# Filling work dealt in another order, with evacuations on either of two engines

## The chip, the core and the metric

The kernel runs on one core of one Trainium2 chip. Its time is the device time of one execution in microseconds (us). Before the change, three runs gave a median of 1594.99 us (1594.81 to 1596.23).

## What is computed

The input `x` has 2048 rows of 512 numbers. Two branches are computed from it and mixed row by row with a gate:

```python
g = _sigmoid((x * gate_w).sum(-1, keepdims=True))
a = _A_ref(x, A_wq, A_wk, A_wv, A_wo)   # attention: 32 query heads of 16, one shared key and value head
b = _B_ref(x, w_gate, w_up, w_down)     # (sigmoid(x @ w_gate) * (x @ w_up)) @ w_down, inner width 1792
return g * a + (1 - g) * b
```

In the attention each query row is compared with all 2048 keys: `softmax(q k / 4) v`, and the heads' results go through `wo`. Branch `b` needs no result of the attention, so its matmuls can be put anywhere between those of the attention; the kernel calls them the filling.

## The kernel before

**Units.** The rows are split in four blocks of 512 (`NB`), and the 32 heads in eight groups of four (`NG`). One block with one group is a unit; there are 32 (`NU`). A unit takes 64 matmuls for the maxima of its scores (`maximum`, L1103, whose result VectorE reduces out of a PSUM bank), 64 for the scores again, the other way up (`scores`, L1112, whose exponential ScalarE takes out of a bank), and 16 value steps (`pv`, L992), each of four narrow matmuls that add exp(scores) times values into one bank.

**The filling.** `block_jobs` (L88) lists it for each block of rows: for each of seven pairs of columns a gate job `g` and an up job `u` (24 matmuls on each half of TensorE), and output jobs `d`, four for each group of pairs in `FG` (L29), that multiply by `w_down`. Jobs `a` multiply the attention result of the block before by `wo`. Before the change the four groups of `d` stand like this: group 0 between `g` and `u` of pair 2 (behind the `a` jobs), group 1 between `g` and `u` of pair 4, groups 2 and 3 in one run at the block's end.

**TensorE in halves.** The matmuls of maxima, scores and filling use 64 rows of the array only; two run side by side, one in the top and one in the bottom half. Such a pair is called a step here. A value step uses the full height.

**The order.** Everything is put in order at build time. `ORDER` (L656) is a text with one sign for each thing that TensorE does next. A hexadecimal digit is a step: its upper and lower two bits say what the top and the bottom half do (0 nothing, 1 a maxima matmul, 2 a scores matmul, 3 a filling matmul). `V` is a value step, `G` a projection group at the start, `T` turns the maxima of a unit, `C` closes the bank of the value sums early, so that the sums go on in another bank, and `.` stands for 25 units of planned waiting. `step` (L624) replays the text in a model, `State`, that keeps a clock for each engine with a table of costs (L40 to L44, in units: a step is 100, a `V` is 371, a reduction on VectorE 260) and so decides at which place the instructions of the other engines, the DMA issues and the GpSimd tasks stand in their queues. Each engine works through its queue in that order; semaphores see to it that nothing is used before it is there.

**Evacuations.** A finished bank is emptied by one engine and then free. Maxima go to VectorE, exponentials, gates and copies to ScalarE, `u` and sums to VectorE. Three things that ScalarE empties matter below: the value sums (`close`, L532, and `sums_out`, L1002: one copy at the end of each unit but the last, which has its own, and one at each `C`); the first part of an output tile, and parts that are added later (`gather`, L432, and `part_of`, L1056: "first" and "apart"). Where a unit's sums come in several copies, GpSimd adds them (`sum_add`, L1005); it also adds the parts that came apart (`add_part`, L1070).

**Buffers.** Eight PSUM banks; two tiles `ou` for the copies of value sums; two buffers `h`; six for the split `hl` (`HB`); four output tiles; two raw buffers for weights on their way in.

Of the kernel before, what the change touches and what calls it, by code (L numbers as in the profile page):

```python
# [11 lines left out]
AF = mybir.ActivationFunctionType  # L12
ALU = mybir.AluOpType
# [8 lines left out]
NT = TB // P  # L22
KC = D // P
# [5 lines left out]
FG = [(0, 2), (2, 4), (4, 5), (5, 7)]  # L29

# [33 lines left out]
M_LEAD, H_LEAD, LOOK = 54, 6, 5  # L64
# [23 lines left out]
def block_jobs(b):  # L88
    out = []

    def ds(gi):
        f0, f1 = FG[gi]
        items = [("d", b, f) for f in range(f0, f1)]
        if gi == len(FG) - 1 and b + 1 < NB:
            items[1:1] = [("x", b + 1, i) for i in range(KC // 2)]
        return [Job("d", b, gi * NT + t, 6 * (f1 - f0), items if t == 0 else ()) for t in range(NT)]

    for gi, (f0, f1) in enumerate(FG):
        for f in range(f0, f1):
            out.append(Job("g", b, f, 24, [("g", b, f)]))  # L100
            if f == f0 and 0 < gi < len(FG) - 1:
                if gi == 1 and b:

                    out += [Job("a", b - 1, t, 3 * KC, [("a", b - 1, i) for i in range(KC // 2)] if t == 0 else ())
                            for t in range(NT)]
                out += ds(gi - 1)
            out.append(Job("u", b, f, 24, [("u", b, f)]))
    return out + ds(len(FG) - 2) + ds(len(FG) - 1)


class State:
# [320 lines left out]
    def gather(self, j, h, i, second, at):  # L432

        key = (j.b, j.i % NT)
        if key not in self.parts:
            self.parts[key] = 1
            n = self.tile_of[key] = self.tile_free.index(min(self.tile_free))
            assert self.tile_free[n] <= self.now
            self.tile_free[n] = NEVER
            self.acts.append(("part", h, j, i, "first"))  # L440
            self.first_at[key] = self.on("act", at, SCALED)
            return self.first_at[key]
        self.parts[key] += 1
# [5 lines left out]
        self.acts.append(("part", h, j, i, "sum"))  # L449
# [6 lines left out]
        return at  # L456

# [74 lines left out]
    def close(self, u, last):  # L532
# [4 lines left out]
        self.acts.append(("sums_out", i, self.sum))  # L537
        at = self.on("act", max(self.now + LATE, self.ou_free[i]), COPY) + TAIL_A
# [142 lines left out]
    "7VV965VVV7a77bf7efededef9bfdbfbf7f6fbdfe7edbbdf6fdV659VV965VVC66f7fe7efbd9fbbfTfff7bfbe7ef7edee7f9ffd5dVVVVC7b7b"
    "7ef6fedbbddbffdfebb7ff6f9fbd6fedffd5dVVVVVC7b7b7e7bfb7bbdbddefb7eb7e7fdefededef9bfdedeVa95VV659VVVCd6fe7ee7fedeb"
    "dbddbfb7ede7fbdeef7bdbff7b7775VVVVVCd9edfef6fe7e7ebd7bfbfTbfb7efdedef9fef977777VVVVC79eefde7f6febdbdfedbdbf9edfe"
    "7fb7bdbf6ff7775VVV6b7b7fb7fbdef9edfed7ddVVVC7adef7bdfbdebd7bfef7dTVVVC66bffdbdf6fbdebd7bfedfefbdfb7fb7ef67ffddaV"
    "VVVVC7b7b97bffedbb7e7fed9feed7fe7edbfe7bf6fafdddVVVVV7b7b7bf9fbdbf6e7fed6fef6ff9bddefe7bedfedf57VVC595VVVC7b7ee7"
    "efdebdbdef7bdbf9fb77efb79fef6bffed9deVV659VV6T9VVC6edf7ebdfbdee7f6f6fbdbdebfdbdfb7bdbedff777aV655VVVV7b7afd7ef9f"
    "6f7bfe7ef9fe7bf6b7ff9defbfeddd5eVVV6a9V9aTVC566VVC7b7bf7bdfbdefeedefdfffedb7efdfef7f7bbV956VVC796ffef9fb7eb7f9ff"
    "dddaVVC5bfb7e7bfbdeede7f6f7ddVVVV7bdef6b7fb7ef9debdf7f7bfbfedeefd9fedbfd77VVVVC66ffbdbdf6febdbdfe7bedfbd6fbdfb7e"
    "dbedff7677VVVa95VVVC6adff7f6fb7bdeedbdfefTefe7bf7edbf9dbfefb77aV95aV555VVVV76b7fbbdfe7eb7f9ef7e7ededfb7bdef9feb7"
    "ffdddaVC6a5VV956VVVC7bde7eb7fb7bf9bdedfefTbfbdfb767efef6fefede5VV95aV969V666V999VVVC79eff67bfbdeede7fede7ef9b7f7"  # L690
    "bbfd6feedff5b7bV95aV59aVV666V996V969V999V666V9a5V9a5V6a9V996VCde6edff6f9fef6fTfbffdbfb7bbdfbde7e7bfff55VVV695VVd"
    "e7e7bb7f9fbf6f9dbf7fb7fbebfdefdededeff57VV656VV6a5VC7a6ff7f6fedaf7fbTfff7bfbedefd9fedef9ff757VVVCde9eedf7fbdbbdd"
    "bf6f777VVCdbb77bfbd9fef6fededd77VVVVC7b7ba7fdfe7afddedefbdef6fbdf6fb7b7e7bfef6ddVVV99aVVVC9bdff6f9fbdbf6bdefd6fe"
    "de7fef6ef7bfTbfbfd775VVVVC766ffeb7fbdeb7dbbfde7b7eb7fe7dbfe7efbddddddVVVVVC5bfe7eedfe7ebd7b7efedebdb7ff9bf7b7b7e"
    "ffddd5VVV6b7ff9f9fedbf67efbd6feVVC7edafdbdfbdebde7fb7e77VV95TVVVC7b6dfeb7fedbf97bfe7f7bffbedf6fedef9f9ff5dVVVVC7"
    "b7ba7fdfedbb7e7e7f9fe7eff6b7f9fedededbff5dVVVVV7bdef6b7fb7bbdbdefdedbedbf77ef6fbdebdef7df9VVC666VV9T5VVC7b7bf9ed"
    "f6fee7edbfdb7bf9f7ef6f9f6fef9fbfd5dVVVVVC7a5ffbb7fedaf7bdf6f9fbf6f7be7efdedbedf9ff5eV965VVVV76efb7defbdef6b7f9f9"
    "fef9fedb7defbdee7fbf577VVV6a9V696V99TVVC7b7bededf9fffbe7bfdfffe7edefdfbfb7ff6VVC6f6f7bbdfb7bf6e7fdddeeVVVCdb9bf7"
    "bdfb7edee7fe7edbVVVV7b7b6fbdfedbdef9fedffbbdefdf9fe7ef6b7fe7bV69aV9a6Va95V6a6Va6aVV9a6VaaaVVaaTVVbaaVVabffebffaf"
    "bVVfeeffbabbbfbcVVeebbbffffffffeeffbfbfebaVVeeaaVVeaeVeeaVaaaVVaaVeeececcceccc8aaV88888VVVV"  # L700
# [11 lines left out]
def tile_kernel(ctx, tc, x_in, wq, wkv, wo, wg, wu, wd, consts_in, out):  # L712
# [289 lines left out]
    def sums_out(i, ps):  # L1002
        nc.scalar.copy(OU[i], ps)  # L1003
# [217 lines left out]
```

## Time and profile before

| what | value |
|---|---|
| median of three runs | 1594.99 us |
| the profiled execution itself | 1595.86 us |
| its span, first to last instruction | 1593.1 us |
| TensorE busy with matmuls | 1585.1 us |
| VectorE busy | 1393.8 us |
| ScalarE busy | 1203.4 us |
| GpSimd busy | 877.9 us |

The profiled execution is 0.87 us above the median, and 2.76 us of it lie outside the span. PE is TensorE, PEld its weight loads, DVE VectorE, ACT ScalarE, POOL GpSimd and SP the engine that issues DMAs. In a list of groups a row gives line, engine, operation, tile written and tiles read, the count, then the time in which any of them ran, the mean duration of one in ns, and after the bar the idle time before them with what ended it. The ends of matmuls are modelled by the profiler; their starts are measured. A maxima, scores or filling matmul is one record; a value step leaves eight records.

### The profile page before, as it was taken

What the parts mean: (1) busy time and instruction counts of PE and PEld (TensorE: products, weight loads), DVE (VectorE), ACT (ScalarE), POOL (GpSimd) and SP (SyncE); (2) the same over time, 40 slices, a digit from 0 to 9 for tenths busy, and PEclk for the clock granted to TensorE, in tenths of its full rate; (3) what the DMA queues carried; (4) which work ended last, traced back from release to release, by engine and by line L of the source; (5) the groups of instructions that cost most, each with busy time, mean ns of one, the idle gap of its engine ahead of it and who ended that gap; (6) DMA issues with size and microseconds to landing.
All of it is one profiled execution on the core that took longest, in us unless ns stands there. A gap on an engine that the chain in (4) does not pass through costs nothing.

```text
span 1593.1 us, 33707 instructions
## 1 busy us (share of the span) xinstructions
PE 1585.1 (99%) x12950; PEld 1001.1 (63%) x12950; DVE 1393.8 (87%) x2420; ACT 1203.4 (76%) x2356; POOL 877.9 (55%) x680
## 2 busy tenths in 40 slices
PE   9999999999999999999999999999999999999998
PEld 7776666556655666665754666666665466666553
DVE  6899999999899998889899989889998998988842
ACT  5277677788788777778778877778778877677797
POOL 5354554666653476567362648285764357656432
PEclk9999999999999999999999999999999999999999
DMA  7312111142111221124011212114211122111011
GB/s 239 139 51 72 39 60 32 32 121 74 38 59 30 77 72 43 34 64 133 27 55 35 72 40 70 36 45 112 84 41 53 32 76 62 51 32 44 9 37 43
DMA packets 52228, 98.10 MB, mean 62 GB/s; under 512 B 17960, under 2 KB 19240, under 8 KB 51044
## 3 DMA queue, kind: packets, MB, share of 16 engines
q1 hardware_dynamic: 52068, 95.96, 20.4%
q8 instruction: 101, 1.65, 0.5%
q14 instruction: 59, 0.48, 0.1%
HBM read 74.05 MB, written 8.90 MB: 52 GB/s over the span
## 4 chain that ended last, share of the span: by engine, by line
PE 99%; ACT 0%; DVE 0%; issue 0%; DVEq 0%; POOL 0%; ACTq 0%; POOLq 0%
PE bank L1087 31%; PE bank L995 30%; PE bank L1108 17%; PE bank L1117 16%; PE bank L849 4%; PE bank L871 0%; ACT p L1119 0%; PE bank L980 0%; PE bank L1160 0%; PE bank L919 0%; ACT x L767 0%; DVE ba L1169 0%; DVEq L1217 0%; POOL v_aug L865 0%; ACT q L941 0%
## 5 line engine op out<-in xcount | busy, mean ns | idle before, releaser
L1110 DVE TENSOR_REDUCE mx<-bank 128x1 f32<-128x512 f32 x2048 | 1261.3, 682 | 133.9 <-PE bank L1108 62.3
L1119 ACT ACTIVATE p<-bank 128x512 f32<-128x512 f32 x2048 | 1043.8, 650 | 85.7 <-PE bank L1117 46.6
L1117 PE MATMUL bank<-qs,ks 64*128 64x512 f32 x2048 | 710.6, 402 | 0.0
L1108 PE MATMUL bank<-ks,qs 62*128 62x512 f32 x2048 | 688.0, 406 | 0.0
L995 PE MATMUL bank<-p,v_aug 128*32 128x512 f32 x4096 | 487.6, 598 | 0.0
L1108 PEld LDWEIGHTS bank<-ks,qs 62*128 62x128 f32 x2048 | 341.1, 185 | 143.7 <-issue 39.2
L1117 PEld LDWEIGHTS bank<-qs,ks 64*128 64x128 f32 x2048 | 352.0, 185 | 107.1 <-DVE mx L1110 33.7
L1087 PE MATMUL bank<-wd,hl 64*128 64x512 f32 x1344 | 265.2, 393 | 0.0
L995 PEld LDWEIGHTS bank<-p,v_aug 128*32 128x32 f32 x4096 | 109.3, 109 | 244.3 <-issue 218.5
L1003 ACT COPY ou<-bank 128x512 f32<-128x512 f32 x112 | 66.2, 591 | 246.3 <-PE bank L995 185.8
L1087 PEld LDWEIGHTS bank<-wd,hl 64*128 64x128 f32 x1344 | 192.3, 185 | 18.9 <-issue 2.5
L1087 PE MATMUL bank<-xs,wu 64*128 64x512 f32 x672 | 188.7, 394 | 0.0
L1087 PE MATMUL bank<-xs,wg 64*128 64x512 f32 x672 | 183.9, 394 | 0.0
L1087 PE MATMUL bank<-x,wu 64*128 64x512 f32 x672 | 183.0, 391 | 0.0
L1087 PE MATMUL bank<-x,wg 64*128 64x512 f32 x672 | 181.6, 391 | 0.0
L1006 POOL TENSOR_TENSOR ou<-ou,ou 128x512 f32<-128x512 f32 x81 | 104.7, 1293 | 137.1 <-ACT ou L1003 136.7
L967 POOL TENSOR_TENSOR qs<-stage,qs 16x1024 fp32r<-16x1024 f32 x62 | 148.4, 2393 | 4.8
L1071 POOL TENSOR_TENSOR ba<-ba,pa_d 128x512 f32<-128x512 f32 x48 | 61.7, 1288 | 116.7 <-DVE ba L1050 77.6
L1087 PEld LDWEIGHTS bank<-x,wg 64*128 64x128 f32 x672 | 112.5, 185 | 10.5 <-issue 0.8
L1087 PEld LDWEIGHTS bank<-xs,wu 64*128 64x128 f32 x672 | 113.1, 185 | 7.9
L1087 PEld LDWEIGHTS bank<-x,wu 64*128 64x128 f32 x672 | 111.7, 185 | 9.6 <-issue 1.7
L1087 PEld LDWEIGHTS bank<-xs,wg 64*128 64x128 f32 x672 | 110.3, 185 | 7.7
(88 smaller groups left out, 1130.1 us busy)
## 6 DMA issues: line engine op xcount, KB each, us to landing
rg<-wg SPq DMA_DIRECT2D x28, 512.0 KB
ru<-wu SPq DMA_DIRECT2D x28, 512.0 KB
rd<-wd SPq DMA_DIRECT2D x28, 512.0 KB
stage<-qd SPq DMA_DIRECT2D x192, 64.0 KB
xs<-x SPq DMA_DIRECT2D x16, 512.0 KB
xf<-x_in SPq DMA_DIRECT2D x16, 256.0 KB
qd<-q SPq DMA_DIRECT2D x16, 256.0 KB
ra<-wo SPq DMA_DIRECT2D x8, 512.0 KB
```

The costliest lines, as they stand in the source:

```text
L849: nc.tensor.matmul(ps, w[:, p, part(kc)], X[b, kc][:, q, :], start=i == 0, stop=i == 3 * KC - 1)
L967: e.tensor_tensor(qs[r], stage[r], f32(qs[r]), op=ALU.subtract)
L995: nc.tensor.matmul(ps[32 * j:32 * j + 32, :], v_aug[:, c, :], PT.pop((u, c, j)), start=new, stop=last)
L1003: nc.scalar.copy(OU[i], ps)
L1006: nc.gpsimd.tensor_tensor(OU[n], OU[n], OU[i], op=ALU.add)
L1071: nc.gpsimd.tensor_tensor(BA[b, t], BA[b, t], PA.pop((b, t)), op=ALU.add)
L1087: nc.tensor.matmul(banks[i], l, r, start=at == 0, stop=at == j.n - 1)
L1108: nc.tensor.matmul(banks[i], qs_t[u % 3][r, pr, part(qt)], ks[r, kb * 512:(kb + 1) * 512], start=True, stop=True)
L1110: nc.vector.tensor_reduce(MX[u][:, pr, h, qt, kb:kb + 1], banks[i], axis=AX.X, op=ALU.max)
L1117: nc.tensor.matmul(banks[i], ks[r, part(c)], qs_t[u % 3][r, pr, :], start=True, stop=True)
L1119: nc.scalar.activation(p, banks[i], AF.Exp, scale=0.25)
```

## The change

Five things change in the planner and in what it emits.

1. `block_jobs` deals the `d` groups by a table `BEHIND`: behind `g` and behind `u` of a pair come two jobs each for groups 1 and 2, all four for groups 0 and 3; the `a` jobs stand behind `g` of pair 2 as before.
2. A function `evacuate` gives the copies of value sums and the "first" and "apart" parts to VectorE or ScalarE, whichever ends earlier by the model's clocks. VectorE's copy is entered with 262 units, its scaled copy with 264; ScalarE's were and are 210 and 247.
3. A copy of value sums is planned to begin 130 units behind the last value step (`LATE_V`), before 190 (`LATE`).
4. `H_LEAD`, by how many matmuls one half of the array may be ahead of the other, goes from 6 to 8.
5. `ORDER` is another text, with the same matmuls. What its signs come to, counted in both texts:

| | before | after |
|---|---|---|
| `V` / `G` / `T` | 512 / 24 / 32 | 512 / 24 / 32 |
| maxima, scores, filling matmuls | 2048, 2048, 4404 | 2048, 2048, 4404 |
| halves that do nothing | 16 | 12 |
| steps (digits) | 4258 | 4256 |
| of these ahead of the first `V` | 108 | 107 |
| runs of `V` | 232 | 230 |
| stretches of steps between runs of `V` | 231 | 229 |
| `C` | 81 | 106 |
| `.` | 0 | 2 |

```diff
+BEHIND = {("g", 2): [(4, 0, 4)], ("u", 2): [(0, 0, 4)], ("g", 4): [(1, 0, 2)], ("u", 4): [(1, 2, 4)],
+          ("g", 5): [(2, 0, 2)], ("u", 5): [(2, 2, 4)], ("u", 6): [(3, 0, 4)]}
...
-M_LEAD, H_LEAD, LOOK = 54, 6, 5
+M_LEAD, H_LEAD, LOOK = 54, 8, 5
+COPY_D, SCALED_D = 262, 264
+LATE_V = 130
...
-    for gi, (f0, f1) in enumerate(FG):
-        for f in range(f0, f1):
-            out.append(Job("g", b, f, 24, [("g", b, f)]))
-            if f == f0 and 0 < gi < len(FG) - 1:
-                if gi == 1 and b:
-
-                    out += [Job("a", b - 1, t, 3 * KC, [("a", b - 1, i) for i in range(KC // 2)] if t == 0 else ())
-                            for t in range(NT)]
-                out += ds(gi - 1)
-            out.append(Job("u", b, f, 24, [("u", b, f)]))
-    return out + ds(len(FG) - 2) + ds(len(FG) - 1)
+    late = [ds(gi) for gi in range(len(FG))]
+    if b:
+        late.append([Job("a", b - 1, t, 3 * KC, [("a", b - 1, i) for i in range(KC // 2)] if t == 0 else ())
+                     for t in range(NT)])
+    for f in range(FG[-1][1]):
+        for kind in "gu":
+            out.append(Job(kind, b, f, 24, [(kind, b, f)]))
+            for gi, first, last in BEHIND.get((kind, f), ()):
+                if gi < len(late):
+                    out += late[gi][first:last]
+    return out
...
-            self.acts.append(("part", h, j, i, "first"))
-            self.first_at[key] = self.on("act", at, SCALED)
+            self.first_at[key], e, _ = self.evacuate(at, SCALED, SCALED_D)
+            self.acts.append(("part", h, j, i, "first", e))
...
-            self.acts.append(("part", h, j, i, "apart"))
-            return self.on("act", max(at, free), SCALED)
+            at, e, _ = self.evacuate(max(at, free), SCALED, SCALED_D)
+            self.acts.append(("part", h, j, i, "apart", e))
+            return at
...
+    def evacuate(self, at, a, d):
+
+        if max(self.dve, at) + d < max(self.act, at) + a:
+            return self.on("dve", at, d), "dve", TAIL + FREE
+        return self.on("act", at, a), "act", TAIL_A + FREE_A
...
-        self.acts.append(("sums_out", i, self.sum))
-        at = self.on("act", max(self.now + LATE, self.ou_free[i]), COPY) + TAIL_A
+        at, e, tail = self.evacuate(max(self.now + LATE_V, self.ou_free[i]), COPY, COPY_D)
+        at += tail - FREE
+        self.acts.append(("sums_out", i, e, self.sum))
...
-        nc.scalar.copy(OU[i], ps)
+        (nc.scalar.copy if e == "act" else nc.vector.tensor_copy)(OU[i], ps)
...
-        nc.scalar.activation(pa, banks[i], AF.Copy, scale=scale[:, n:n + 1])
+        if e == "dve":
+            nc.vector.tensor_scalar(pa, banks[i], scale[:, n:n + 1], None, op0=ALU.mult)
+        else:
+            nc.scalar.activation(pa, banks[i], AF.Copy, scale=scale[:, n:n + 1])
```

The text of `ORDER` (some 4900 signs) is left out of the diff; so are lines that only pass the engine's name on.

More of the change, by code (lines that the diff above doesn't have):

```diff
@@ L446, in gather @@
             self.halves[j.key, "slot"] = slot
-            self.acts.append(("part", h, j, i, "apart"))
-            return self.on("act", max(at, free), SCALED)
-        self.acts.append(("part", h, j, i, "sum"))
+            at, e, _ = self.evacuate(max(at, free), SCALED, SCALED_D)
+            self.acts.append(("part", h, j, i, "apart", e))
+            return at
+        self.acts.append(("part", h, j, i, "sum", "dve"))
         at = self.on("dve", max(at, self.first_at[key]), SUM)
@@ L697 @@
[L697 to L700, printed above, removed]
+    "GGGGGGGG555G555G555G555GG555GG555GGG555GG555G555G555Gdd55GTfffdf777ff7f777ffffffefb7edbf7b7f9fb7efdef79ffedbe7de"
@@ new lines @@
+    "fbde7bbdfed9feffff55VVVC9deefdededefedf6efdb7bdedfdff777777VVVVC97bbfdbdbf77bf7befdedee7fede7ededeffd577VVVC7bTf"
+    "bfb7bfb7b7bfb7e7bdbfb7df577VVVC9dbb7f7bdfdedefbfdbdeff777775VVV6ededfededbfbdedfe7ede7ef6fe7bff55.VVVC6de7bf9fb7"
+    "7bfbffddddd5VVVVC9dedededefeff7f6fb7b7bfeeefTffb7bf767ef77VVC9b7b7b77bfbedfdfdeddddVVVVC6ede7f6fb7edbff6fb7b7ef9"
+    "bf79fbf9f6fedffddd5VVV956VVC97bf9fb7bbdedfedbf7b7e7eedf6febde7f9fefff5TVVVVVC7b76b7fbfbd9fbe7def9fb7bf9ff9edfede"
+    "f6fedf5dVVVVC67b7bbfdb7bedff7fede7e7efbfededfbdef6ff57VVVVV6edef76fbf6efddebf7b7b7b7bfb7afdb7fefededddVVVC6f6def"
@@ new lines @@
+    "edb7b7efbdb7f6fdVV999VVC7e7bf6f6fedb7bedbfdfdTVVVC6deeeddfef6f9ff9dbf6fee7b7fbdef9dbff7bb7777V99aV666V699V659VV6"
+    "eddbfb7b7ddVVC6b7bfdbd7ddeVVC6deedfbdbbdfbddbfbededfb76fefedbdbfe77777VVV67baV95aV9a5V6TaV696VC6f9bfdbdfd7aVVC9d"
+    "eedfeb77b7VVded9bffb79f6fbdefe7b7e7b7ef7ef6f9feb7ffde5dVVC655VVVC6b6ffdedeb7b7fefdefTbfb7bf7b9fededfe7efeb57VV6a"
+    "5V999V699V996V65aV65aV999V656VV9deeddbfde7efeeffb7b7bfbfb7b7e7bfbdffdd5dVVVC69edffedeedfe7f77b7efedebffb7bfdbfbd"
+    "f7757VVVVVC9b77bfe7bdbe7fe7f9fe7beddbfeeTffe7bf7fdedd5VVVVC97bfb7edef9f6f9fedfedef6fbd9fb7ef6f9fff5777VVVV6f6fbd"
@@ new lines @@
+    "9fbf6b7f9ffed6fef9fb7edef75VVC9e9ff76fff5aVVVVCdadff67bfb7bdbedfedb7ef6f7eb7ef7edbf9ff6f5dVVVaaTVVVC9bdfb7bdbf9f"
+    "b77bedfedef9fe7edbbdfedb76fff6dV9a9V696V669V969V666VC699V669VC669V66aV6a5V996V95aV966VCdeTeeff7bf9b7f9f6fed77VVC"
+    "9b77bf9fef9dbf7efed7ddVVVV9e9ffdedef9fbdb7ffde7bfeedefde7ff7b7b7777VVVVC97bfbdb7b7efe76fe7fedbf9def6faf7def9fedf"
+    "f75VVVC7bTbfef9ff9b7fbd9fedddVVVC6b7fe7b7b7bfe7bffb7be7e7e7fefb67VVVC9f9fedb7bf9ef7e7fe7fdddddVVV9e6f7fede7eeVVV"
+    "C99ffb7b7edbbfd7bfe7edeedfede7af7fffddd5VVVVCTeedeffd6f6efedf9fbb7bdfbdededb7bfb7bffb775VVVVC67b7bfe7bb7fb77efe7"
@@ new lines @@
+    "edef6f9f6fedbfdbfdfdddd5VVVVV67b7b7efb7fe7bfdf9f9fbdefbfde7efe7ef7ddddVVVVC6b77bbdfbbdf9fedefdedede7bfbe7deedfbf"
+    "e7b777VVVVC97bfb7efTbfb7bfedeedddVVC97bfb7b7b7eefdeddeffdaV966V666V559VVV7e7ef9f6f6fbde7ebf7ededb7efb7b7fbdbdbdb"
+    "fdddVVC9defb76fe77dVVVC9ededfb7d77bVVC6edf6feb7bdfed7bfb7ef9f6ef7bdbdbb7fbdeffeTdVVC9edfe7bdf775VVV65aVC6b7fedbd"
+    "ebfaVVV9bdfb7bdef9fe7edf9fedef9edfe7af7e7fb7bf5fffed5VVVVVC96f7bf9fb7bb7fededfedede7efedbdbfbb7b777VV666V95aV6Ta"
+    "V696VC95aV65aV696VC67bfe7e7ebddbf9fbfdffedbdef9ffededf7bb777VV9deeeddfbedfdfb7777777VVVVC9b7bf7edbf6bdfbf7ddeddV"
@@ new lines @@
+    "VVC67bfbde7edefedbdbdfb7bb7fb7e7e7efbdedefTff5VVVVVC7b7e7bf9f9f9fe7efe79fef9feddefe7edef7b7bf57VVVVd6fedebdfbd6f"
+    "bdbf6fedbf9dbfedbdfb7ed7f77777VVVVVCTbfedefe7b7bbdf9fb7e7fed9fb7bfe7bbdedfedef6VV996V669V956VVVC9b77ef9fedeedfde"
+    "b7f9fbb7bf7edbf6f9fb76fefddV69aV9a5V669V699V696VC669V969VC966V666VC666V9a5VTa9V9a5VC9f9fbd9fbdee7fe7fb76fdVVC97b"
+    "fb7ededeb7f6fef77ddVVVV9ededfb7ef9bf7dbf9fffededefedef7f7b7b7777VVVVC9b7bb7b7bfdfe7e7fededef9f9feeTffbdbfdb7efd5"
+    "VVVVC6b7b7fb7be7f6fbfbfdb7be7ef79faf7VVVC9e6ff7e7e7efededeffee7edfededf57VV959VVV6dbdbfb7bf7b7bfddededdVVVC67ef6"
@@ new lines @@
+    "f6febddfedebfdbdbdedbfbf9f9e7fff777775VVVVC97bfb79fbf9fede7f9fbfTbfedefdadff6defef7577VVVVC9b7fb7edeedf6fdefedbd"
+    "ef6bdfbdbdbf7e7bff7775VVVVV6b97ffed7be7bff9fed7fbebff7e7fedeedb7f7ddVVVVC97bfededbb7bf7eeddfbededfe7be7f9fedbfe7"
+    "7777VVVVC97efb7edb7bfbddedeffbTVVC9b7fe7e7e7b7bfdeffded5VVVVC9e9f7fb7be7e7fdbe7fbdef6fe7b7eededfb7bdf7ddVV9ede7f"
+    "bdbb7dVVC696V6a5VC97af7fbdbeeeVV9T5VVC7e6fdbdefedef6b7fbd6fbdbbdfb7fedb7bf9fbfed5VVVVC97edef6feb7bVVC9ededefb777"
+    "bVV6f6f6fef6e7edfedfbd9fbbdfb7bdbedbfde7bf5f77VVC655VVVCd9efdebdfbdbb7fb6fdef9fededf6fbdbedbfbb7777VV65aV6a5V9Ta"
@@ new lines @@
+    "V95aVC666V95aV6a5V659VV66ff9f9ff9dbfb7bf7def7bfbfe7efe7ef6e7fdddVVVVC6b7fbd9fef9e7f7bfedffbfbdb7fefTeefdefd677VV"
+    "VVC6deedfb7ef9bfddebfdb7b7bf9fb7ededef9fff7b75VVVVVC97bbfdedbdbfb7edfe7e7ef6f6f9fb7bedfed9fef77VV6a5V655VVVC6ded"
+    "efede7b7efedfb7bdbb7fb7b79feef7edef7fb5V96TVVVVC6f9edfe7edebfddbf9fb7b7bf9fbdedbe7fe7f7ff55VVVVVC9f6fbd9fbf9defd"
+    "bf6f6fbde7efb7bb77bfedefdfd6VC969V966V666V669V699VC699VC65aV669V95aV9TaV966V95aVC97b7bb7bbf7fbf7bdbfe7ef9f6fb7fe"
+    "5VVVC9dedefe7ef6deffbfed9fbf9ffdddddVVV6edededfeedff77b7b7b77VVVVC9f9fb7e7ef6f6f6fbf7b7bbfd6fef6defb7efdeefd5VVV"
@@ L701 @@
+    "b7ef67ef9fbf9dbdbf9fe7bdefedfed6fbf6efd777VVC559VVVC9e9ff7bb7bfTfef6fdf9fadfededfedbf6fefb7b7b5VVVC97e7ef6fef9fb"
+    "ddeff7757VVVVC69f7bf9fe7e7bff9fbf9fefeb7fbdededefedf6bV6b57VVV99fbf7b7bf6ef76feefeee4VC6a6V996V69aV9a9V9a9Vaaa.V"
+    "Va9aVVaTaVaaaVVaaVeeeeeVVbbbffbffbfbbbffbffeeffbbbbaVVaabVVebfeffefefbbbffeaVVeaeeeceVVaaa8VVVVeeeeecccecee8V888"
+    "8VVV"
 )
@@ L1000, in tile_kernel, with sums_out @@
     SUMS = {}
[L1002 to L1003 removed]
+    def sums_out(i, e, ps):
+        (nc.scalar.copy if e == "act" else nc.vector.tensor_copy)(OU[i], ps)
     def sum_add(_, i, n, last):
@@ L1054, in send_out, with part_of @@
         nc.sync.dma_start(out[n * P:(n + 1) * P, :], BA.pop((b, t)))
-    def part_of(h, j, i, how):
+    def part_of(h, j, i, how, e):
         b, t = j.b, j.i % NT
```

45 lines of the change are left out of this document (5 added, 40 removed).

## The prediction

> **What bounds the kernel now.** I read the page's head, its busy row and its chain first, then the list of waits of PE alone.
>
> ```profile
> span 1593.1 us, 33707 instructions
> ...
> PE 1585.1 (99%) x12950; PEld 1001.1 (63%) x12950; DVE 1393.8 (87%) x2420; ACT 1203.4 (76%) x2356; POOL 877.9 (55%) x680
> ...
> PE 99%; ACT 0%; DVE 0%; issue 0%; DVEq 0%; POOL 0%; ACTq 0%; POOLq 0%
> ```
>
> ```profile
> PE bank L871 <- POOL v_aug L865: 1.3, 1, 1.3
> PE bank L1146 <- ACT ou_last L1144: 0.5, 1, 0.5
> PE bank L1155 <- DVE on L1153: 0.4, 1, 0.4
> ```
>
> The chain is TensorE for 99% of the span, and PE's own waits come to 2.2 us, all at the two ends. That alone doesn't settle it: ends of matmuls are modelled, so a short stall can hide in a busy PE. So I price TensorE's work from starts. The next rows are pieces of the chain (start, length): runs of value steps, eight records a step.
>
> ```profile
> 93.52 3.57 PE bank L995 x32
> 107.09 4.43 PE bank L995 x40
> ...
> 1159.76 2.71 PE bank L995 x24
> 1163.37 2.71 PE bank L995 x24
> ```
>
> A run of five steps takes 4.43 us and one of four 3.57: 0.86 us a `V`, and 4.43 - 5 x 0.86 = 0.13 us to get into a run. Between the first two lie 107.09 - 97.09 = 10.00 us. In the text of `ORDER` the first two runs of `V` have 42 steps between them, without a `T`. Between the last two lie 0.90 us, where the text has three steps. A step is (10.00 - 0.90) / 39 = 0.233 us, and getting out of a run costs 0.90 - 3 x 0.233 = 0.20 us. The rows below are windows: the length, then the busy time and count of PE, PEld, DVE, ACT and POOL, clock, DMA share, GB/s.
>
> ```profile
> 97.09:107.09 10.00, 10.00 (x88) 8.14 (x92) 9.60 (x17) 8.64 (x17) 7.18 (x8) 1.00 0.29 91
> 107.09:111.52 4.43, 4.43 (x42) 1.20 (x42) 3.27 (x6) 0.60 (x1) 4.20 (x4) 1.00 0.10 38
> 1162.47:1163.37 0.90, 0.90 (x11) 0.50 (x14) 0.17 (x1) 0.44 (x1) 0.87 (x1) 1.00 0.00 0
> 0.00:93.52 93.52, 92.12 (x497) 71.59 (x501) 72.91 (x133) 41.06 (x72) 38.00 (x30) 1.00 0.54 171
> 93.52:1583.53 1490.01, 1489.68 (x12443) 928.17 (x12443) 1317.85 (x2281) 1160.52 (x2279) 838.64 (x650) 1.00 0.19 54
> 1583.53:1593.14 9.61, 3.29 (x15) 1.37 (x14) 3.06 (x7) 1.86 (x5) 1.27 (x1) 0.90 0.29 109
> ```
>
> The last three cut the span into the head up to the first `V`, the body, and the end behind the last `V`. The body, by the counts of the old text: 512 x 0.86 = 440.3 us, 232 runs x 0.13 = 30.2, 4150 steps (4258 less 108 in the head) x 0.2333 = 968.2, 231 stretches x 0.20 = 46.2. That is 1484.9 of 1490.0. The 5.1 us left hold 31 `T` and every stall there is. **TensorE hardly waits for anyone; the time is the count of its work**, and whatever the other engines gain is worth at most those 5 us.
>
> **The change, part by part.** *The new order on TensorE.* The matmuls are the same. In the body, two runs of `V` and two stretches go, 2 x (0.13 + 0.20) = 0.66 us, and one step (4150 to 4149), 0.23; in the head one step more, 0.23. Two signs `.` come in; at 100 units to a step of 0.233 us, 25 units are 0.06 us each, so 0.12. Sum: -0.66 - 0.23 - 0.23 + 0.12 = **-1.0 us**. `T` and `G` keep their counts. The weights' loads and GpSimd's splits keep theirs and stand elsewhere in their queues; SP's later DMAs stand behind them. I cost this at nothing: the DMA share of the body is 0.19. If that cover failed, TensorE, in order, would stand until the weights are split; no such wait is in its list now.
>
> *More closes.* `C` goes from 81 to 106. With 31 unit ends that makes 137 copies of value sums for 112, and 106 adds on GpSimd for 81.
>
> ```profile
> L1110 DVE TENSOR_REDUCE mx<-bank 128x1 f32<-128x512 f32 x2048 | 1261.3, 682 | 133.9 <-PE bank L1108 62.3 <-PE bank L1087 45.7 <-PE bank L1117 22.1
> ...
> L1006 POOL TENSOR_TENSOR ou<-ou,ou 128x512 f32<-128x512 f32 x81 | 104.7, 1293 | 137.1 <-ACT ou L1003 136.7
> ...
> L1003 ACT COPY ou<-bank 128x512 f32<-128x512 f32 x112 | 66.2, 591 | 246.3 <-PE bank L995 185.8 <-issue 31.2 <-DVE ba L1050 4.3
> ```
>
> ```profile
> L1068 ACT ACTIVATE pa_d<-bank,gom x48: 687/767/888, 228.9 to 1524.1; 128x512 f32<-128x512 f32 x48
> L1068 ACT ACTIVATE ba<-bank,gom x16: 687/760/853, 142.8 to 1311.7; 128x512 f32<-128x512 f32 x16
> L1068 ACT ACTIVATE pa_a<-bank,gsig x16: 687/794/995, 501.6 to 1561.3; 128x512 f32<-128x512 f32 x16
> ```
>
> 25 adds x 1.293 = 32.3 us more on POOL, which is idle for 1593.1 - 877.9 = 715 us, and 25 x 0.591 = 14.8 us on ACT or DVE. Both lie beside TensorE: nothing. If POOL were the bound, the 32.3 us would be the price. A copy must also wait for one of two `ou` tiles; behind it in its engine's queue wait the next reductions or exponentials, and for their banks TensorE.
>
> *Either engine.* At most 137 copies and 48 + 16 + 16 = 80 scaled parts can move to DVE, 217 in all (in the fence above: count, then shortest, median and longest in ns). No row shows a 128x512 copy on DVE. The nearest are a reduction, which also reads 512 columns of a bank, at 0.682 us (2048 of them keep DVE busy for 1261.3 / 2048 = 0.616 us each), and the subtraction L773, whose two operands lie in SBUF:
>
> ```profile
> L773 DVE TENSOR_TENSOR x<-xf,x x8: 675/685/1617, 4.6 to 16.4; 128x512 fp32r<-128x512 f32 x8
> ```
>
> ```profile
> 12.19 2.54 POOL L898 TENSOR_TENSOR wq<-wqr,wq 128x512 fp32r<-128x512 f32 x2 [1.66 <-ACT wq L895]
> 13.67 3.42 DVE L773 TENSOR_TENSOR x<-xf,x 128x512 fp32r<-128x512 f32 x4 [2.69 <-ACT x L767]
> ```
>
> Its median is 0.685, its longest 1.617 us. The second fence shows one place where it is slow: four take 3.42 us from 13.67, though POOL's two subtractions end at 14.73; 3.42 - 4 x 0.616 = 0.96 is about the 1.06 us by which POOL was still running. Ends for a copy: 0.682 and 1.617. I take the reduction, since it reads the same bank; the planner's 262 units are 0.61 us (100 to a step of 0.233), its spacing of 0.616. So at most 217 x 0.616 = 134 us move to DVE, which is idle for 1593.1 - 1393.8 = 199 us. The window of the five-step run shows where, 3.27 busy of 4.43, and the copies fall at the ends of runs. Between runs there is less: 9.60 of 10.00. I cost it at nothing; were DVE full everywhere, it would be the whole 134 us.
>
> *The copy planned earlier.* 130 units are 0.30 us behind the last value step, 190 were 0.44. The rows of the run from 107.02 and of one from 268.37, each with its copy:
>
> ```profile
> 107.02 4.50 PE L995 MATMUL bank<-p,v_aug 128*32 128x512 f32 x40
> ...
> 111.58 0.59 ACT L1003 COPY ou<-bank 128x512 f32<-128x512 f32 x1 [3.86 <-PE bank L995]
> ```
>
> ```profile
> 268.37 2.78 PE L995 MATMUL bank<-p,v_aug 128*32 128x512 f32 x24
> ...
> 271.27 0.59 ACT L1003 COPY ou<-bank 128x512 f32<-128x512 f32 x1 [1.50 <-POOL hl L742]
> ```
>
> 111.58 - 107.02 - 5 x 0.86 = 0.26 us, and 271.27 - 268.37 - 3 x 0.86 = 0.32 us. The new entry lies between: the old one held a reserve of 0.12 to 0.18 us, the new one -0.02 to +0.04. If each of 137 copies frees its bank 0.02 us late and TensorE waits for each, that is 2.7 us; I take 0 and keep 2.7 for the range. `H_LEAD` adds no instruction.
>
> The sum is -1.0 us: 1595.86 - 1.0 = 1594.9 for an execution like the profiled one, and, 0.87 lower, **1594.0 us** for the median.
>
> **The rivals.** *Stalls go too (faster).* Of the 5.1 us left over, some are stalls; a plan with VectorE's help might lose them. For: L1003 holds up to 246.3 us of ACT's idle time. Against: none of it shows on PE, and 31 `T` need part of the 5.1. If 2.5 us of it go, 1591.5. To be outside 0.2% (3.2 us below 1594.99, which is about what a measurement of this kernel can tell from no change) more than 2.2 us must go. Chance 0.05.
>
> *VectorE is held up by GpSimd (slower).* The wait of L773 beside L898 may meet any operation of DVE that writes or reads SBUF in bulk, so the new copies too. POOL is busy for 55%, and a copy that meets one of its 1.29 us operations waits for half of it on average: 0.55 x 0.65 = 0.36 us each. The reserve of a stretch (0.40 us in the window from 97.09) is used up at the second of them; from there each delays a reduction, its bank and TensorE. With half of the 217 moved, 109 x 0.36 = 39 us of lateness, and half of that in such stretches: +19 us less 1.0, 1613; if only the 80 parts do it, 40 x 0.36 x 0.5 = +7, so 1601. Against:
>
> ```profile
> L1097 DVE SCALAR_TENSOR_TENSOR h<-gs,bank 128x512 f32<-128x512 f32 x56 | 38.0, 679 | 1.2 <-PE bank L1108 0.4
> ```
>
> These read a bank and one SBUF tile and write 512 columns to SBUF, spread over the whole span beside POOL, and take 0.679 us on average: no excess over a reduction. A copy reads less. Chance 0.09. The Trainium skill, in "SBUF — State Buffer", section "SBUF: two separate sides", has this as an exclusive lock between GpSimd and a VectorE operation that uses two ports or has two inputs in SBUF; "VectorE: DVE Perf Modes", section "Mode 2×_2P", closes the two-port mode to an operand in PSUM. By these pages L773 is locked out, as the trace has it, and the new copies are not: +0. No run here shows the copy itself.
>
> *The change moves no evacuation.* The model's rule may find ACT earlier nearly always. Then only the counts act: 1594.0 again, so it shares the forecast's place. Chance 0.10.
>
> **How the numbers follow.** Forecast 0.76 and the rival that gives the same time 0.10: within 0.2% with 0.86. Faster 0.05; slower 0.09. The range reaches up by the 2.7 us of late banks and 1 us for the spread of the runs before (0.18 below to 1.24 above the median), to 1597.7, and down by 2 us of stalls gone, to 1592.0. The slower rival and the end of the faster one stay out, under 0.2 together.
>
> **What would show it.** Right: 137 copies on L1003's successor, shared by ACT and DVE; 106 adds, POOL near 910 us busy; the pieces 0.86, 0.13, 0.233 and 0.20 us unchanged; a body near 1489.1 us with no new row in PE's own waits; a DVE copy near 0.68 us. Wrong: a body over 1492 us with the same pieces, that is, TensorE standing, with PEld waits on DVE or on `hl` that are new; DVE copies with a long tail over 1 us, as in L773. A different price of a step would break the whole count.

## The result and the profile after

The changed kernel takes 1593.02 us (median of 20 runs, 1592.13 to 1594.11). The kernel before takes 1595.38 us in the runs beside it (20 runs, 1594.43 to 1596.23). The ratio is 0.9986, with a 95% interval of 0.998 to 0.9992: 2.4 us faster, or 0.14%, which is a real difference and a smaller one than the 0.2% within which the prediction counts a time as the same. The profiled execution took 1592.79 us.

The page of the changed kernel: its head, its busy row and its chain.

```profile
span 1591.0 us, 33696 instructions
...
PE 1582.7 (99%) x12950; PEld 1008.2 (63%) x12950; DVE 1406.1 (88%) x2443; ACT 1194.6 (75%) x2358; POOL 909.2 (57%) x705
...
PE 99%; DVE 0%; DMA 0%; ACT 0%; SPq 0%; issue 0%; DVEq 0%; ACTq 0%
```

The list of PE's own waits, the same view as before:

```profile
PE bank L886 <- POOL v_aug L880: 1.3, 1, 1.3
PE bank L1164 <- ACT ou_last L1162: 0.5, 1, 0.5
PE bank L1173 <- DVE on L1171: 0.4, 1, 0.4
PE bank L864 <- ACT x L782: 0.2, 1, 0.2
```

The bound is the same. POOL has 25 operations and 31 us more, DVE 23 operations and 12 us more, ACT 9 us less, and the chain is still TensorE alone. The list of waits holds nothing new in the body. It would not have shown the gain either.

The windows of the changed kernel (columns as in the prediction): the head up to the first `V`, the body, and the end.

```profile
0.00:93.55 93.55, 91.81 (x496) 71.15 (x500) 72.40 (x132) 40.98 (x72) 38.42 (x30) 1.00 0.54 171
93.55:1581.26 1487.71, 1487.62 (x12445) 935.71 (x12444) 1330.60 (x2305) 1151.76 (x2281) 869.50 (x675) 1.00 0.19 54
```

The span fell by 1593.14 - 1591.0 = 2.1 us. With the body before cut in the same way (first `V` to the end of the last),

```profile
93.52:1583.58 1490.06, 1489.68 (x12443) 928.17 (x12443) 1317.85 (x2281) 1160.52 (x2279) 838.64 (x650) 1.00 0.19 54
```

the body gives 1487.71 - 1490.06 = -2.35 us, the head +0.03, and the end the rest, +0.2. So the gain lies in the body, and the prediction's count can be laid beside it: 512 x 0.86 = 440.3, 230 runs x 0.13 = 29.9, 4149 steps x 0.2333 = 968.0, 229 stretches x 0.20 = 45.8, together 1484.0. Of the body's 2.35 us the count explains 1484.9 - 1484.0 = 0.9. The leftover, turns and stalls, went from 5.2 to 3.7 us: **1.5 us of the gain are time in which TensorE stood before and doesn't stand now.**

What was evacuated by whom is in the groups of the changed kernel:

```profile
L1128 DVE TENSOR_REDUCE mx<-bank 128x1 f32<-128x512 f32 x2048 | 1258.7, 680 | 121.9 <-PE bank L1126 80.7 <-PE bank L1135 33.4 <-PE bank L1105 4.2
...
L1021 POOL TENSOR_TENSOR ou<-ou,ou 128x512 f32<-128x512 f32 x106 | 137.1, 1293 | 138.1 <-ACT ou L1018 135.1 <-DVE ou L1018 2.4
...
L1018 ACT COPY ou<-bank 128x512 f32<-128x512 f32 x135 | 79.5, 589 | 291.8 <-PE bank L1010 213.1 <-issue 37.4 <-POOL ba L1089 8.2
...
L1084 DVE TENSOR_SCALAR pa_d<-bank,gom 128x512 f32<-128x512 f32 x13 | 9.6, 741 | 0.0
...
L1084 DVE TENSOR_SCALAR pa_a<-bank,gsig 128x512 f32<-128x512 f32 x5 | 3.7, 748 | 7.5 <-PE bank L1105 7.5
...
L1084 DVE TENSOR_SCALAR ba<-bank,gom 128x512 f32<-128x512 f32 x3 | 2.2, 741 | 0.0
...
L1018 DVE COPY ou<-bank 128x512 f32<-128x512 f32 x2 | 1.4, 690 | 8.1 <-PE bank L1010 8.1
```

Only 13 + 5 + 3 + 2 = 23 of the 217 evacuations that could move did move. A copy takes 0.690 us on VectorE, a scaled part 0.741 to 0.748.

**Where a stall sits.** Take one stretch without a `T` in each kernel, both of 43 steps by their texts, so 0.20 + 43 x 0.2333 = 10.23 us by the count. Pieces of the chain (start, length), before and then after:

```profile
408.47 2.71 PE bank L995 x24
421.61 4.43 PE bank L995 x40
```

```profile
205.94 4.43 PE bank L1010 x40
...
220.64 3.57 PE bank L1010 x32
```

Before: 421.61 - (408.47 + 2.71) = 10.43 us, 0.20 over the count. After: 220.64 - (205.94 + 4.43) = 10.27, 0.04 over. The timeline of before, inside its stretch (start, length, instruction, in brackets the wait and what ended it):

```profile
414.48 0.39 PE L1117 MATMUL bank<-qs,ks 64*128 64x512 f32 x1
414.72 0.18 PEld L1108 LDWEIGHTS bank<-ks,qs 62*128 62x128 f32 x1 [0.29 <-ACT p L1119]
414.72 0.50 PE L1108 MATMUL bank<-ks,qs 62*128 62x512 f32 x1
...
415.07 0.39 PE L1117 MATMUL bank<-qs,ks 64*128 64x512 f32 x1
```

From 414.48 to 415.07 are 0.59 us for two steps that take 0.47: 0.12 us lost. A maxima matmul needed the bank that an exponential (L1119) was still emptying. PE shows no wait; its weight load, PEld, does. Such waits of PEld are no measure of the loss by themselves, since most of them lie under the matmul that is still running (one row of the changed kernel's list alone holds 40.9 us, its whole leftover is 3.7); only the distance of starts tells what was lost.

This stretch is one of the two worst without a `T`. More is lost at the turns of the maxima themselves. PEld's waits for a bank at the line of the turns (total us, times, longest), before and then after:

```profile
PEld bank L980 <- ACT p L1119: 2.7, 6, 0.5
```

```profile
PEld bank L995 <- ACT p L1137: 0.9, 2, 0.4
```

One of the six in the timeline of before:

```profile
775.21 0.43 PE L1087 MATMUL bank<-x,wg 64*128 64x512 f32 x2
...
775.70 0.12 PEld L980 LDWEIGHTS bank<-consts,mm 64*16 64x16 f32 x2 [0.50 <-ACT p L1119]
775.74 0.22 PE L980 MATMUL bank<-consts,mm 64*16 64x64 f32 x2
```

From 775.21 to 775.74 are 0.53 us for one step of 0.23: 0.30 us lost, because the turn (L980) needed a bank that an exponential was still emptying.

### The profile page after: what moved, and what is told of

The parts are those of the page before. It is cut to its first block, busy times and chain, and to the rows that moved or that the text cites. A ratio compares the mean times of both kernels' runs of the same rounds, so it can differ in the third digit from the quotient of the medians.

```text
span 1591.0 us, 33696 instructions
## 1 busy us (share of the span) xinstructions
PE 1582.7 (99%) x12950; PEld 1008.2 (63%) x12950; DVE 1406.1 (88%) x2443; ACT 1194.6 (75%) x2358; POOL 909.2 (57%) x705
## 4 chain that ended last, share of the span: by engine, by line
PE 99%; DVE 0%; DMA 0%; ACT 0%; SPq 0%; issue 0%; DVEq 0%; ACTq 0%
PE bank L1105 32%; PE bank L1010 30%; PE bank L1135 17%; PE bank L1126 16%; PE bank L864 3%; DMA xf<-x_in 0%; DVE mx L1128 0%; PE bank L995 0%; PE bank L1178 0%; ACT x L782 0%; PE bank L934 0%; SPq L767 0%; DVE ba L1187 0%; DVEq L1235 0%; ACT q L956 0%
## 5 line engine op out<-in xcount | busy, mean ns | idle before, releaser
L1135 PE MATMUL bank<-qs,ks 64*128 64x512 f32 x2048 | 730.9, 405 | 0.0
L1126 PEld LDWEIGHTS bank<-ks,qs 62*128 62x128 f32 x2048 | 346.4, 185 | 121.8 <-DVE mx L1128 40.9
L1018 ACT COPY ou<-bank 128x512 f32<-128x512 f32 x135 | 79.5, 589 | 291.8 <-PE bank L1010 213.1
L1105 PE MATMUL bank<-wd,hl 64*128 64x512 f32 x1344 | 271.6, 391 | 0.0
L1021 POOL TENSOR_TENSOR ou<-ou,ou 128x512 f32<-128x512 f32 x106 | 137.1, 1293 | 138.1 <-ACT ou L1018 135.1
L1105 PEld LDWEIGHTS bank<-wd,hl 64*128 64x128 f32 x1344 | 201.6, 185 | 15.6
L1105 PE MATMUL bank<-xs,wu 64*128 64x512 f32 x672 | 182.6, 392 | 0.0
```

What stands on the lines that cost most here:

```text
L1018: (nc.scalar.copy if e == "act" else nc.vector.tensor_copy)(OU[i], ps)
L1021: nc.gpsimd.tensor_tensor(OU[n], OU[n], OU[i], op=ALU.add)
L1105: nc.tensor.matmul(banks[i], l, r, start=at == 0, stop=at == j.n - 1)
L1126: nc.tensor.matmul(banks[i], qs_t[u % 3][r, pr, part(qt)], ks[r, kb * 512:(kb + 1) * 512], start=True, stop=True)
L1135: nc.tensor.matmul(banks[i], ks[r, part(c)], qs_t[u % 3][r, pr, :], start=True, stop=True)
```

## The experiments

The first two are the two kernels again, without an edit.

> The kernel before, profiled a second time. Theory (the gain beyond the count comes from short stalls that the new order no longer has): the stretches of steps between runs of value steps again exceed their count (0.2331 us a step, 0.199 a stretch, 0.09 a turn of the maxima) by about 2.5 us in the body, as in the first profile, and stretches that hold a turn again carry over half of it. Rival (one profile's luck): the excess differs from profile to profile by 1 us or more, and the extra gain is not the order's. Time equal to the kernel before.

> The changed kernel, profiled a second time. Theory: the excess of the stretches over their count is again near 0.9 us, 1.5 us under that of the kernel before; body near 1488.2 us. Rival (luck): it comes out anywhere between 0.5 and 2.5 us. Time about 0.9985 of the kernel before.

Measured: 1595.26 us, ratio to before 1.0001 (0.9992 to 1.001), and 1592.88 us, ratio 0.9986 (0.9977 to 0.9995). The bodies, first of the old kernel and then of the new:

```profile
93.61:1583.98 1490.37, 1489.96 (x12444) 927.11 (x12443) 1317.97 (x2281) 1160.63 (x2279) 839.43 (x650) 1.00 0.19 54
```

```profile
92.98:1580.18 1487.20, 1487.13 (x12444) 933.00 (x12444) 1331.09 (x2305) 1150.44 (x2281) 870.37 (x675) 1.00 0.19 55
```

The leftovers are 1490.37 - 1484.9 = 5.5 and 1487.20 - 1484.0 = 3.2 us. They repeat within 0.5 us; the second body of the changed kernel is 1.0 us shorter than the 1488.2 that was expected. The drop between the two kernels is 1.5 us in the first pair of profiles and 2.3 in the second. The second profile of the changed kernel is the fastest of its 11 runs, 1591.82 us, so 2.3 is the high end: the medians, 2.4 and 2.2 us apart, leave 1.5 and 1.3 beyond the count. The places repeat too: in the second profile of before, the stretch at 408.5 us stands by the same amount and at the same weight load.

```profile
414.88 0.18 PEld L1108 LDWEIGHTS bank<-ks,qs 62*128 62x128 f32 x1 [0.29 <-ACT p L1119]
```

The excess over the count, in the sense of the expectations, is 2.5 and 2.8 us before and 0.9 and 0.5 after: it doesn't differ from profile to profile by the rival's 1 us or more, and in the kernel before the stretches with a turn carry over half of it both times (the table further down). These stalls are built into the order; they are no noise.

**All 23 back on ScalarE**, in the same order and at the same places of the queues:

```diff
-        (nc.scalar.copy if e == "act" else nc.vector.tensor_copy)(OU[i], ps)
+        nc.scalar.copy(OU[i], ps)
...
-        if e == "dve":
+        if False:
```

> The changed kernel with its order and its places in the queues, but all 23 evacuations that went to VectorE are issued on ScalarE. Theory (the gain is the order's): the time of the changed kernel, within 0.5 us, 0.9985 of the kernel before. Rival (the gain beyond the count is VectorE's help): the 1.3 us beyond the count are lost again, 0.9993 of the kernel before.

Measured: 1599.9 us, ratio to before 1.0031 (1.0019 to 1.0042). That is 7.0 us more than the changed kernel beside it, 0.30 us on average for each evacuation put back, and the expectation missed it by far. The body holds nearly all of it, 1494.55 - 1487.71 = 6.8:

```profile
93.85:1588.40 1494.55, 1494.38 (x12445) 933.60 (x12444) 1318.36 (x2282) 1163.34 (x2304) 870.39 (x675) 1.00 0.19 54
```

The timeline at one of the 23:

```profile
378.82 0.70 ACT L1086 ACTIVATE pa_d<-bank,gom 128x512 f32<-128x512 f32 x1
...
379.58 0.18 PEld L1135 LDWEIGHTS bank<-qs,ks 64*128 64x128 f32 x1 [0.19 <-ACT pa_d L1086]
...
380.07 0.29 PEld L1105 LDWEIGHTS bank<-wd,hl 64*128 64x128 f32 x3 [0.30 <-ACT p L1137]
380.07 0.50 PE L1105 MATMUL bank<-wd,hl 64*128 64x512 f32 x2
...
380.41 0.39 PE L1105 MATMUL bank<-wd,hl 64*128 64x512 f32 x1
```

The part on ScalarE delays the exponentials behind it, their banks are late, and the next matmuls stand, first for the part itself and then for an exponential. In the changed kernel, at that place, ScalarE goes through its exponentials without a gap and VectorE takes the part beside them:

```profile
375.93 4.12 ACT L1137 ACTIVATE p<-bank 128x512 f32<-128x512 f32 x8
...
377.98 0.74 DVE L1084 TENSOR_SCALAR pa_d<-bank,gom 128x512 f32<-128x512 f32 x1
```

**All 217 on VectorE**, the opposite:

```diff
-        (nc.scalar.copy if e == "act" else nc.vector.tensor_copy)(OU[i], ps)
+        nc.vector.tensor_copy(OU[i], ps)
...
-        if e == "dve":
+        if True:
```

> The changed kernel with all 137 copies of value sums and all 80 scaled parts issued on VectorE in the same places, 194 more than the 23 that went there. VectorE gets 194 x 0.616 = 120 us more, to about 1526 of 1591 us. Theory of the prediction (a copy out of a bank costs VectorE what a reduction costs, no lock against GpSimd): copies at a mean near 0.69 us with no tail over 1 us; TensorE waits only where VectorE is already full, 0.2 to 0.4 us at each of some 99 long stretches, so 20 to 40 us slower than the changed kernel, 1.011 to 1.024 of the kernel before. Rival (held up by GpSimd): a mean over 1.0 us with a tail to 1.6, and 60 us or more slower, over 1.037.

Measured: 1649.31 us, ratio 1.0341 (1.0326 to 1.0355), 56 us over the changed kernel. For 194 evacuations more on VectorE that is 0.29 us each on average: the size of the lateness that was seen on ScalarE, now on the other engine. The time lies between the theory's 20 to 40 us and the rival's 60, nearer to the rival's, so the durations have to decide (shortest, median, longest in ns):

```profile
L1018 DVE COPY ou<-bank x137: 626/691/695, 96.2 to 1604.2; 128x512 f32<-128x512 f32 x137
```

```profile
L1084 DVE TENSOR_SCALAR pa_d<-bank,gom x48: 728/739/752, 235.2 to 1577.8; 128x512 f32<-128x512 f32 x48
```

No tail. A lock by GpSimd, of the kind supposed from L773's 1.617 us, would have shown as copies of over 1 us; none of the 137 is longer than 0.695, with POOL busy for 55% of the span. What grew is the number of waits for a bank that VectorE reduces. PEld's waits (total us, times, longest), first in the changed kernel, then here:

```profile
PEld bank L1126 <- DVE mx L1128: 40.9, 51, 0.8
PEld bank L1135 <- DVE mx L1128: 31.4, 38, 0.8
```

```profile
PEld bank L1135 <- DVE mx L1128: 67.2, 161, 0.8
PEld bank L1126 <- DVE mx L1128: 63.3, 116, 0.8
```

277 times for 89: the reductions stand behind the evacuations in VectorE's queue. The slowdown is a queue that is too full, not a slow operation.

**114 runs of `V` more**, with the same signs otherwise (`x` stands for a step; as the planner replays this text, 22 evacuations go to VectorE, not 23):

```diff
-xVVx   (at 114 places)
+VxVx
```

> The changed kernel with 114 runs of value steps more (344 for 230): where a run of two or more follows a step, the last step changes places with the first value step. Same matmuls, same closes. Theory (the time is the count: 0.13 us into a run and 0.20 us out of it): 114 x 0.33 = 37.6 us slower than the changed kernel, 1630.5 us, 1.022 of the kernel before. Rival (a switch costs little by itself, since the other engines catch up in it): under 20 us slower, below 1.012.

Measured: 1631.41 us, ratio 1.0226 (1.021 to 1.0242), 38.4 us over the changed kernel's 1593.02; 114 x 0.33 = 37.6 was the count. The body,

```profile
93.74:1619.29 1525.55, 1525.43 (x12446) 918.30 (x12446) 1336.37 (x2305) 1153.99 (x2282) 870.35 (x675) 1.00 0.18 53
```

leaves 1525.55 - 1521.8 (440.3 + 344 x 0.13 + 4150 x 0.2333 + 343 x 0.20; one step of the head now stands behind the first `V`) = 3.7 us, as in the changed kernel. The price of a run holds for 114 runs as for the two of the change.

**15 early closes less** (15 of the signs `C` taken out of `ORDER`, so 15 copies and 15 adds less; here too 22 evacuations go to VectorE):

> The changed kernel with 15 of its 106 early closes taken out (91 left), all else in its order; 15 copies and 15 adds on GpSimd fewer. Theory (copies and adds lie beside TensorE): the time of the changed kernel within 0.5 us, 0.9985 of the kernel before. Rival (a copy on ScalarE delays the exponentials behind it, 0.3 us each as the 23 evacuations moved back to ScalarE did): 15 x 0.3 = 4.5 us faster than the changed kernel, 0.9958.

Measured: 1593.71 us, ratio 0.9992 (0.9983 to 1.0001), 0.7 us above the changed kernel's 1593.02, a little more than the 0.5 that the theory allowed and within the spread of the runs. The rival's 4.5 us faster is far off. The extra closes cost nothing that can be seen; taking some away doesn't help.

**The old order, evacuations on either engine.** On the kernel before, 15 scaled parts go to VectorE by the model's rule; the model's clocks still count them on ScalarE, so that everything else stays where it was.

```diff
-            self.acts.append(("part", h, j, i, "first"))
+            self.acts.append(("part", h, j, i, "first", self.pick(at, SCALED, SCALED_D)))
...
+    def pick(self, at, a, d):
+        return "dve" if max(self.dve, at) + d < max(self.act, at) + a else "act"
```

> The kernel before, in its old order and with its old places in the queues, but with the choice of the engine for evacuations: the model's rule, asked without letting its clocks change, moves 15 scaled parts (3 first, 12 apart) and no copy to VectorE. Theory (TensorE's short stalls in the old order are waits for banks that ScalarE frees late): part of them goes, 0.5 to 1.5 us faster than the kernel before, 0.9991 to 0.9997. Rival (each evacuation on VectorE delays its reductions as in the run with all of them there, 0.29 us each): 15 x 0.29 = 4.4 us slower, 1.0027.

Measured: 1599.53 us, ratio 1.0025 (1.0015 to 1.0036), 4.4 us more than before, 0.29 us for each of the 15. The rival was right and the theory fell: VectorE's help, laid over an order and a plan that weren't made for it, takes no stalls away. The old order with a planner whose clocks know of the choice was not run. The body:

```profile
93.71:1588.03 1494.32, 1493.51 (x12444) 924.69 (x12443) 1327.32 (x2296) 1154.99 (x2264) 839.48 (x650) 1.00 0.19 54
```

One of the 15 in the timeline:

```profile
536.67 0.74 DVE L1073 TENSOR_SCALAR ba<-bank,gom 128x512 f32<-128x512 f32 x1
...
537.33 1.28 DVE L1117 TENSOR_REDUCE mx<-bank 128x1 f32<-128x512 f32 x2
537.41 0.38 PE L1124 MATMUL bank<-qs,ks 64*128 64x512 f32 x1
...
538.07 0.18 PEld L1115 LDWEIGHTS bank<-ks,qs 62*128 62x128 f32 x1 [0.66 <-DVE mx L1117]
538.07 0.49 PE L1115 MATMUL bank<-ks,qs 62*128 62x512 f32 x1 [0.22 <-DVE mx L1117]
...
538.40 0.39 PE L1124 MATMUL bank<-qs,ks 64*128 64x512 f32 x1
```

VectorE takes the part, its next two reductions begin only when it is done, at 537.33, and the next maxima matmul waits for the bank of one of them: from 537.41 to 538.40 are 0.99 us for two steps, 0.52 lost. The picture of the 23 put back on ScalarE, with the engines exchanged.

**ScalarE alone, but planned so.** Here the planner itself may not choose, so its clocks know where the evacuations are. Its rules then ask for 96 signs `.` more in the new order, 96 x 25 = 2400 units, or 5.6 us:

```diff
-        if max(self.dve, at) + d < max(self.act, at) + a:
+        if False:
```

> The changed kernel with the choice of the engine taken out of the planner too: all 217 evacuations go to ScalarE, its clock knows it, and 96 signs of 25 units of planned waiting stand in the order, which is otherwise the same. Other than in the run with only the instructions moved, every task and DMA now stands where a planner without the choice puts it. Theory (the 23 evacuations make banks late on ScalarE in this order, wherever the rest stands): 96 x 25 units = 5.6 us and up, as with the instructions moved: 1598.5 to 1600.5 us, 1.002 to 1.0035 of the kernel before. Rival (the loss of 7 us came from queues that no longer fitted their plan): under 2 us slower than the changed kernel, below 1.000.

Measured: 1598.58 us, ratio 1.0018 (1.0009 to 1.0027), at the lower end of what the theory said (1598.5 us and, by the ratio, 1.002). That is 5.6 us more than the changed kernel, as much as the waiting that was planned. A `.` issues no instruction; what makes the time are the late banks that the planner foresaw, for the run with only the instructions moved lost 7.0 us without these signs. The body is 1492.91 us with the same matmuls and runs, so the leftover is 1492.91 - 1484.0 = 8.9 us:

```profile
93.84:1586.75 1492.91, 1492.85 (x12444) 934.51 (x12444) 1317.95 (x2282) 1163.02 (x2304) 869.99 (x675) 1.00 0.19 54
```

**ScalarE alone, in an order made for it.** The same edit, and `ORDER` improved by small exchanges of neighbouring signs until the plan came to 1025 units, 2.4 us, over the changed kernel's (91 `C`, 43 `.`, 4256 steps, 230 runs):

> The same without the choice of the engine, and with the new dealing of the output groups, but the order's signs changed by a search of small exchanges until the planned waiting was down from 2400 units to 1025 over the changed kernel's plan; 91 closes, 43 signs of waiting, as many steps and runs. Theory (the time is the order as long as each evacuation stands where the order has room for it): 1025 units = 2.4 us above the changed kernel, 1595.4 us, 1.0002 of the kernel before. Rival (an evacuation on ScalarE costs 0.3 us in any order): 1599 us or more, 1.0025.

Measured: 1595.69 us, ratio 1.0001 (0.9992 to 1.001). The theory's 1595.4 holds and the rival's 1599 and more falls: an order without VectorE's help can be had at the old kernel's time. This text of `ORDER` also has 15 `C` less than the changed kernel's.

None of these kernels is faster than the changed one.

## Why the prediction was right, and where it was not

**What bounds the kernel: right.** The chain, the list of waits and the pieces of 0.86 us a `V` are as they were, and the run with 114 more runs puts the count's price on a firm footing.

**The count, -1.0 us: right where it can be told.** The body's -0.9 comes from it. The -0.23 of the head isn't to be seen: the head took 93.52 before and 93.55 after, but over the runs here it lies between 92.98 and 93.85, so a step is below what it can show. The +0.12 for two `.` is too small to see in this change. For the time as a whole the forecast was -1.0 us and the change -2.4; that 1593.02 lies so near to 1594.0 is in part luck, since the kernel before came out 0.4 us higher in the runs beside it than the 1594.99 that I started from.

**"The 5.1 us left hold 31 `T` and every stall there is": right, and the step that was mis-sized.** I took the change of that term as 0. It measured -1.5 us in one pair of profiles (5.2 to 3.7) and -2.3 in the other (5.5 to 3.2). Laid over the stretches one by one (each stretch's length less 0.199 and 0.2331 a step, and less 0.09 for each `T`, which is what a turn comes to in the changed kernel), the excess sums to 2.5 and 2.8 us in the two profiles of before and to 0.9 and 0.5 in the two of after. The rival "stalls go too" was thus right in its mechanism, with 1.5 to 2.3 us for the 2.5 that it supposed. I gave it little because none of ScalarE's lateness showed in PE's own waits; it stood in those of PEld, and in the distances of starts.

The traces also show where these stalls went, and by what. Below is the excess over the count of the 31 stretches that hold a turn, and of all others, in us, taken from the start of each run of `V` to the start of the next (so the sums are 0.1 to 0.2 us lower than those just given).

| kernel | with a turn | without |
|---|---|---|
| before, in its two profiles | 1.4 and 1.5 | 0.9 and 1.2 |
| changed, in its two profiles | 0.2 and 0.1 | 0.7 and 0.3 |
| changed, 23 back on ScalarE | 0.2 | 7.5 |
| changed order, planned for ScalarE alone | 0.2 | 5.9 |
| an order made for ScalarE alone | 0.3 | 3.3 |
| old order, 15 parts on VectorE | 2.1 | 4.5 |

Most of the drop, 1.3 us in the first pair and 1.4 in the second, lies at the turns. It is there in the three kernels with all evacuations on ScalarE too, and it isn't there with the old order and VectorE's help. So the new order, with the plan that goes with it, took these stalls away, and not the choice of the engine. What VectorE's help does is something else: it keeps the new order from losing 5 to 7 us in the other stretches.

**More closes cost nothing: right.** 137 copies and 106 adds are there, POOL is at 909.2 for my 910, and with 15 closes less nothing was won.

**Either engine at no cost: right for the time, wrong as a reason.** A copy takes 0.690 us for my 0.682. But I argued from idle time of the whole span, 199 us on VectorE and more on ScalarE. By that reasoning the 23 could stand on either engine, and 15 parts of the old order could move. Both cost about 0.3 us an evacuation on average, and with all 217 on VectorE, the number that I priced at nothing because 134 us fit into 199, the kernel is 56 us slower. That the term came to nothing in the time rests on how few the planner moved, and I didn't foresee that. Only 23 of 217 moved, so the third rival, that nothing moves, was nearly right in number, and wrong about what the few are worth in their order: with the 23 issued elsewhere the time is 7 us longer.

**The plan behind the last value step, 2.7 us kept for late banks: not needed.** The leftover fell. No run has the earlier copies alone.

**VectorE held up by GpSimd: wrong.** 217 evacuations ran beside GpSimd and none took over 0.76 us, with GpSimd busy for 55% of the span. The Trainium skill, "SBUF — State Buffer", section "SBUF: two separate sides", puts the lock on VectorE operations with two ports or two inputs in SBUF; the copies read PSUM, and the 0.695 us of their longest agrees with it.

**Together.** The order and the choice of engine belong to one plan. With the choice laid over the old order it is 4.4 us slower than before; with the new order and everything issued on ScalarE it is 4.8 slower than before, or 3.2 slower where the planner knows of it; with an order made for ScalarE alone, the same as before; with both, 2.4 faster. What stays open is how much of what the order gained is due to the dealing of the output jobs, how much to the text of `ORDER`, and whether `H_LEAD` and `LATE_V` have a part in it: no run has any of them alone. It is also open whether a longer search without the choice would reach the changed kernel's time.

## What to carry to other kernels

Where one engine is busy for 99% of the span, count its work with prices taken from starts and look at what is left over; short stalls are there, and not in that engine's busy share or its list of waits. Idle time of another engine over the whole span says nothing on whether it can take one more operation at a given place: here a misplaced evacuation of 0.6 to 0.75 us cost 0.3 us on average on either engine, with each of them idle for over 180 us. When work moves to another engine, the plan that sets the order must know of it.

## What was not expected of the hardware

In the places looked at, a late bank cost more than its wait. The first step behind a wait takes longer than the 0.233 us of a step: 415.07 - 414.72 = 0.35 us in the kernel before, 380.41 - 380.07 = 0.34 with the 23 on ScalarE, 538.40 - 538.07 = 0.33 with 15 parts on VectorE. In the run with all 217 on VectorE, 171 steps in stretches without a turn start together with a weight load that had waited; the median distance to the next step is 0.337 us there, and 0.231 for the other steps. In all three places the weight load starts at the time that the matmul shows, rather than ahead of it; that the 0.10 to 0.12 us are this load, no longer hidden, is the likely reading and was not tried alone. A scaled part reads and writes as much as a copy and takes 0.05 us longer on VectorE (0.741 to 0.690).
